# Attention and gated feed-forward on one core: the third query tile of two neighbouring head pairs by seven products over two query blocks

## The chip, the core and the metric

The kernel runs on one core of a Trainium2 chip. A core has a matrix engine (TensorE, PE in the profile, with its weight loads as PEld), a vector engine (VectorE, DVE), a scalar engine (ScalarE, ACT), a general engine (GpSimd, POOL) and a queue engine (SyncE, SP) that issues most transfers. The matrix engine writes its products to PSUM, eight banks of 512 float32 values in each of 128 partitions; everything else lies in SBUF or in the chip's main memory.

The metric is the device time in microseconds of one execution. A change is measured as the ratio of the times of the two kernels on the same chip.

## What is computed

`x` is 2048 rows of 640. It is normalized by rows (`xn`). Attention has 32 heads of width 192 and reads the last 512 rows of the key and value caches. The feed-forward part has a hidden width of 1536. Cut to what matters:

```python
xn = _layernorm(x)                                  # 2048 x 640
q = (xn @ wq).reshape(B, Sq, 32, 192)               # 32 heads
scores = einsum("bhqd,bhkd->bhqk", q, k[-512:]) * 192 ** -0.5
o = einsum("bhqk,bhkd->bhqd", softmax(scores), v[-512:])
s = o.reshape(B, Sq, 32 * 192) @ wo                 # 6144 x 640
g = silu((silu(xn @ w_gate) * (xn @ w_up)) @ w_down)
out = x + s * g
```

## The kernel before, in words

The work has three stages in time. First the feed-forward part over four blocks of 512 rows (to about 165 us), with the layer norm, the preparation of `wo` and of the first head pair beside it. Then the attention over 16 pairs of heads (to about 690 us). Then the output projection. The order of every engine's instructions is the order in which the code emits them: the scheduler is switched to manual.

**Attention.** Two heads have 384 columns of queries, that is three tiles of 128 columns (j = 0, 1, 2) for each of four blocks of 512 rows. A head pair has two halves of two blocks each. Each half is a *scores phase* (`scores_phase`) and a *stretch* of value products (`stretch`). A scores phase has eight slots. Each slot holds one group of six score matmuls (`scores`, L780, into one of two score tiles of two PSUM banks, read by an exponential on ScalarE, L789) and, ahead of it, some of the work that makes the queries of the *next* two blocks: blocks 2 and 3 of the same pair in the first half, blocks 0 and 1 of the next pair in the second. That work comes in units of ten matmuls of 64 rows by 512 columns; two of them run side by side in the two halves of the array. The products of a unit go to one of two tiles of two banks (`mm_tile`).

The first two query tiles of two blocks are not made by four products each (two row halves of `xn` by two column halves of the weights, for two blocks) but in the manner of Winograd's form of Strassen's scheme: seven products for eight. `q_diag` (L736, one unit for both groups of a pair), `differences` (L751), `sides` (L757), `across` (L763) and `sums` (L771) are its steps; the weights' sums come from `combine_wq` (L152, VectorE at L174, copies on GpSimd at L176 to L178), the sums of `xn` are made once (`xc`). One of the additions runs on GpSimd (L769). The third tile (j = 2) is made directly by `q_rows` (L711): two partial products over 64 rows each, which VectorE adds (L722). So a half has three units for the first two tiles and two for the third, and the first half has the diagonal unit of the next pair as a sixth, in slot 7.

Beside the slots (`beside`, L1060) go the transposes of the next pair's keys, their sums (`sum_k`, L200) and their centring (`centre_k`, L209 and L211), the loads of the pair after that (`load_k`, `load_wq`), and the spill of finished outputs to main memory (L868). The value products (L824) are divided on VectorE and ScalarE (`divide`, L847 and L853) and transposed by DMA (L859).

**The down projection** (`ffn_down`, L442) takes two row tiles at a time, also by seven products (W1 to W7) in three PSUM banks U, V, W out of four, which lie two by two in two tiles.

**The output projection** (`run`, L985) does the same with products M1 to M7 for eight pairs of row tiles; the last operations are products M3 into the bank of M5, two VectorE operations and a store.

Of the kernel before, what the change touches and what calls it, by code (L numbers as in the profile page):

```python
# [15 lines left out]
def kernel(  # L16
# [114 lines left out]
    BLOCKS = (slice(0, 6, 5), slice(2, 4), slice(1, 5, 3))  # L131
# [19 lines left out]

    def combine_wq(pr, step=0):  # L152

        rows = pairs[pr]["rows"]
        if step == 0:
            pairs[pr]["wq"] = wpool.tile([P, 5, NC, P], bf, name="wq_p", tag="wq_p")
        w = pairs[pr]["wq"]
        wc = pairs[pr]["wc"] = w[:, :, :, :].bitcast(h16)

        def part(of, r, n, t):  # L160
            return of[r, n, :, BLOCKS[t], :]

        def slot(of, r, n):
            return of[r, n, :, :].rearrange("p c (b d) -> p c b d", d=64)

        if pr == 0:
            for t in range(3):
                nc.vector.tensor_copy(out=slot(w, full, AS_IS[t]), in_=part(rows, full, 0, t))
            return
        if step < 2:  # L170
            r, own, other = ((lo, 1, 0), (hi, 0, 1))[step]
            a, b, c = part(rows, r, 0, own), part(rows, r, 0, other), part(rows, r, 1, other)
            for to, x, y, op in ((SWAP, c, a, ALU.add), (TOTAL, c, b, ALU.add), (OTHER, b, a, ALU.subtract)):
                nc.vector.tensor_tensor(slot(wc, r, to), x, y, op)  # L174
        else:
            nc.gpsimd.tensor_copy(out=slot(w, full, THIRD), in_=part(rows, full, 0, 2))  # L176
            nc.gpsimd.tensor_copy(out=slot(w, lo, OWN), in_=part(rows, lo, 0, 1))
            nc.gpsimd.tensor_copy(out=slot(w, hi, OWN), in_=part(rows, hi, 0, 0))  # L178

# [22 lines left out]
    CENTRE = [(0, lo, 0, lo), (0, hi, 2, hi), (1, full, 1, full), (2, lo, 0, hi), (2, hi, 2, lo)]  # L202
# [20 lines left out]
    def q_of(i, j):  # L223
        return q_pair(i)[:, 3 * (i % 2) + j, :]
# [4 lines left out]
    with ExitStack() as fctx:  # L229
# [212 lines left out]
        def ffn_down(b, u):  # L442
# [3 lines left out]
            at = 3 * (2 * b + u)  # L446
            U, V, W = (down_banks[(at + k) % 4] for k in range(3))
# [250 lines left out]

    pre = ctx.enter_context(tc.tile_pool(name="out_first", bufs=1, side="right"))
    ictx = ctx.enter_context(ExitStack())  # L700
    ppool = ictx.enter_context(tc.tile_pool(name="att_p", bufs=10, side="right"))
    opool = ictx.enter_context(tc.tile_pool(name="att_o", bufs=2, side="right"))
    otpool = ictx.enter_context(tc.tile_pool(name="att_ot", bufs=4, side="right"))
# [22 lines left out]
    DIAG_S, SIDE_S = 0, 1  # L726
# [9 lines left out]
    def q_diag(pr):  # L736

        ps, wc = mm_tile(), pairs[pr]["wc"]
        products(ps, [wc[:, SWAP, :, :]] * 2, [xc[:, DIAG, :, :]] * 2)
        nc.vector.tensor_copy(out=m_f[:, DIAG_S, :, :], in_=ps[:, :, :])  # L740

    def q_group(pr, g):
# [3 lines left out]
        st = {}  # L746

# [3 lines left out]
        def differences():  # L751
            st["own"] = mm_next[0]
            st["ps"] = mm_tile()
            w = pairs[pr]["wq"][:, OWN, :, :]
            products(st["ps"], [w] * 2, [xc[:, DIFF[g], :, :]] * 2)

        def sides():  # L757
            side = mm_tile(1 - st["own"])
            wc = pairs[pr]["wc"][:, TOTAL, :, :]
            products(side, [wc] * 2, [block(1), block(0)])  # L760
            nc.scalar.copy(m_f[:, SIDE_S, :, :], side[:, :, :])  # L761

        def across():  # L763
            nc.vector.tensor_tensor(  # L764
                q_pair(i)[:, 1:4:2, :], st["ps"][:, :, :], m_f[:, SIDE_S, ::-1, :], ALU.add
            )
            diag = m_f[:, DIAG_S, g : g + 1, :].to_broadcast([P, 2, 512])
            eng = nc.vector if pr == last else nc.gpsimd
            eng.tensor_tensor(m_f[:, SIDE_S, :, :], diag, m_f[:, SIDE_S, :, :], ALU.subtract)  # L769

        def sums():  # L771
            wc = pairs[pr]["wc"][:, OTHER, :, :]
            products(st["ps"], [wc] * 2, [xc[:, SUM[g], :, :]] * 2, first=False)
            nc.vector.tensor_tensor(
                q_pair(i)[:, 0:5:4, :], st["ps"][:, :, :], m_f[:, SIDE_S, :, :], ALU.add
            )

        return differences, sides, across, sums, lambda b: q_rows(i + b, 2, 1 - st["own"])
# [29 lines left out]
    def pv(i, q2, tile_of, by_dve):  # L808
# [3 lines left out]
        def part(p):  # L812
            if p == 0:
                if i not in OTs:
                    Obs[i] = O_late.pop(0) if i >= NS - 2 else opool.tile([P, 4, 2, Dh], bf, name="O_b")
                    OTs[i] = otpool.tile([P, 12, P], bf, name="OT_b")
# [89 lines left out]
    def load_a(n, q, cs=slice(0, KH), eng=nc.sync):  # L906
        side, k = divmod(q, 2)
        if (n, q) not in a_q:
            if n > 2 and n % 2:
                a_q[n, q] = a_q[n - 2, q]  # L910
            elif n == 1 and k == 0:
                pool, tag = ((wpool, "wq_p"), (wstage, "wq_rows"))[side]
                a_q[n, q] = pool.tile([P, KH, P], bf, name="a_q", tag=tag)
            else:
                pool = pre if n % 2 == 0 else wide
                a_q[n, q] = pool.tile([P, KH, P], bf, name="a_q", tag="a_q%d" % q)
# [8 lines left out]
    def a_sum(n, m):  # L925
        x, y, op = A_OF[m]
        third = len(a_s) % 3 == 2
        a_s[n, m] = (late[0] if third else qpool).tile(
            [P, KH, P], h16, name="a_s", tag="a_s" if third else "qT", bufs=1 if third else 2
        )  # L930

        def part(q):
            return a_s[n, q][:] if q in A_OF else a_q[n, q][:]

        nc.vector.tensor_tensor(a_s[n, m][:], part(x), part(y), op)

    def product(n, m, ps, first=True, ns=1):
        at = a_s[n, m] if (n, m) in a_s else a_q[n, A_OF[m][0]]
        w = HC // ns
        for k in range(ns):  # L940
            for c in range(KH):
                nc.tensor.matmul(  # L942
                    ps[k] if ns > 1 else ps, at[:, c, :], b_w[m][:, c, k * w : (k + 1) * w],
# [3 lines left out]
    def load_xg(n):  # L947
        for side, r in enumerate(ROW_PAIRS[n]):
            tag, bufs = ("khat", 2) if n % 2 == 0 else (("K_p", "KT")[side], 1)
            t = xg[n, side] = kpool.tile([P, 2, D], bf, name="xg", tag=tag, bufs=bufs)  # L950
# [34 lines left out]
    def run(n, m):  # L985
# [17 lines left out]
        elif m == M5:  # L1003
            ps = bank(n, "M5+M3")
            product(n, M5, ps)
            total(v, ps, v)
# [16 lines left out]
        else:  # L1023
# [4 lines left out]
            product(n, M3, ps, first=False)  # L1028
            if (n, m) == ORDER[-1]:
                total(c, ps, t[:, 1, last_cols], ALU.mult)  # L1030
                total(t[:, 0, last_cols], c, u)
                store(n, 0, last_cols, nc.scalar)
            else:
                total(u, ps, u)
# [12 lines left out]
        "0a0 s20 0b0 s21 0a1 s22 0b1 s23 1a0 s30 1b0 s31 1a1 s32 1b1 s33 "  # L1047
        "2a0 2b0 2a1 2b1 3a0 3b0 3a1 3b1"
# [11 lines left out]
    def beside(pr, n):  # L1060
# [11 lines left out]
        elif pr + 2 < NPAIR and n in (10, 12):  # L1072
            (load_k if n == 12 else load_wq)(pr + 2)
        half, n8 = divmod(n, 2 * KC)
# [21 lines left out]
    def scores_phase(pr, half):  # L1096


        nxt = pr + 1 < NPAIR
        if half == 0 and pr == 0:  # L1100
            work = [lambda i=i, j=j: q_rows(i, j) for i in (2, 3) for j in range(3)]
            slots = {0: work[0:1], 1: work[1:2], 3: work[2:3], 4: work[3:4], 5: work[4:5], 6: work[5:6]}
        elif half == 0 or nxt:
            of = pr if half == 0 else pr + 1
            differences, sides, across, sums, third = q_group(of, 1 - half)
            slots = {
                0: [differences], 1: [sides], 3: [across, lambda: third(0)], 4: [sums],
                6: [lambda: third(1)],
            }
        if half == 0 and nxt:  # L1110
            slots.setdefault(7, []).append(lambda: q_diag(pr + 1))
# [92 lines left out]
```

## Time and profile before

| what | us |
|---|---|
| median of three runs | 878.79 (878.28 to 879.32) |
| the profiled execution | 878.91 |
| its span, first to last instruction | 877.1 |
| TensorE clock granted | 1.00 throughout |
| PE busy, first stage (0 to 150) | 145.6 of 150 |
| PE busy, attention (300 to 600) | 299.9 of 300 |
| PE busy, end (800 to 877) | 73.5 of 77 |

The profile shows one execution. Busy time of an engine is the union of its instructions; since matmuls are pipelined, a busy PE is not PE at its peak. Durations of PE instructions include the way through the array, so that groups overlap; the pace is read from the starts. In lines of the timeline the columns are start, duration, engine, line, operation, tiles (out<-in), shapes and count, and in brackets the engine's idle time before it and what ended it.

### The profile page before, as it was taken

Reading aid. Unit: us, or ns where it says so; the run is one execution under the profiler, and the core shown is the slowest. Engines: PE = TensorE matmul, PEld = TensorE weight load, DVE = VectorE, ACT = ScalarE, POOL = GpSimd, SP = SyncE. Lnnn points to the kernel's source line nnn. Section 1 sums busy time; section 2 is a strip of 40 time slices with the busy share of each in tenths; the row PEclk is TensorE's granted clock in tenths of the full one; section 3 lists DMA queues with packets and bytes.
Section 4 is the critical chain, followed back from the end, with each engine's and each line's share of the span. In section 5 each row is a group of like instructions: output and inputs, shape, how many; then the busy total and the mean of one; then the engine's idle time right before and its main releaser. Section 6 shows DMA issues by size and latency. Waiting matters only on the chain.

```text
span 877.1 us, 22922 instructions
## 1 busy us (share of the span) xinstructions
PE 867.6 (99%) x9641; PEld 576.2 (66%) x9657; DVE 603.5 (69%) x1028; ACT 427.5 (49%) x649; POOL 114.2 (13%) x217
## 2 busy tenths in 40 slices
PE   8999999999999999999999999999999999999998
PEld 5455555567667667667667667667667777777775
DVE  6765876676876876876876876877775556555553
ACT  4264433665765765765765765765767300000000
POOL 0000000112122122122122132132120000000000
PEclk9999999999999999999999999999999999999999
DMA  9669974258999988977987777978899998645510
GB/s 294 172 210 275 214 222 116 67 98 180 204 204 217 201 179 200 195 162 176 198 177 179 176 149 163 208 165 189 167 230 251 255 355 294 212 171 176 176 54 16
DMA packets 273432, 165.52 MB, mean 189 GB/s; under 512 B 174384, under 2 KB 268208, under 8 KB 272816
## 3 DMA queue, kind: packets, MB, share of 16 engines
q1 hardware_dynamic: 271824, 156.08, 73.8%
q10 hardware_dynamic: 1504, 7.96, 2.6%
q8 instruction: 76, 1.25, 0.6%
q14 instruction: 28, 0.23, 0.1%
HBM read 89.95 MB, written 40.24 MB: 148 GB/s over the span
## 4 chain that ended last, share of the span: by engine, by line
PE 96%; DMA 1%; SPq 1%; DVE 1%; issue 0%; ACT 0%; ACTq 0%; DVEq 0%
PE acc L942 19%; PE sc L785 18%; PE mm L731 13%; PE sc L394 11%; PE mm L824 10%; PE sc L824 9%; PE mm L717 8%; PE mm L456 5%; PE sc L523 1%; DMA OT_b<-O_last 1%; DMA wg_sb<-in_B_w_gate_dram 1%; PE gu L394 0%; SPq L921 0%; DVE wq_p L174 0%; SPq L859 0%
## 5 line engine op out<-in xcount | busy, mean ns | idle before, releaser
L789 ACT ACTIVATE p_t<-sc 128x1024 bf16<-128x1024 f32 x256 | 253.6, 1024 | 59.8 <-PE sc L785 55.2
L785 PE MATMUL sc<-qT,khat 64*128 64x512 bf16 x1536 | 198.1, 376 | 0.0
L824 PEld LDWEIGHTS <-p_t 64*128 64x128 bf16 x4096 | 173.0, 94 | 8.6
L785 PEld LDWEIGHTS <-khat 64*128 64x128 bf16 x1536 | 89.0, 94 | 75.2 <-issue 0.5
L824 PE MATMUL mm<-V_p,p_t 64*128 64x193 bf16 x2112 | 111.6, 243 | 0.0
L824 PE MATMUL sc<-V_p,p_t 64*128 64x193 bf16 x1984 | 104.8, 243 | 0.0
L731 PE MATMUL mm<-xc,wq_p 64*128 64x512 f16 x750 | 94.4, 376 | 0.0
L942 PEld LDWEIGHTS <-a_s 128*128 128x128 f16 x768 | 75.1, 98 | 29.2
L731 PEld LDWEIGHTS <-wq_p 64*128 64x128 f16 (+1 forms) x1050 | 58.4, 94 | 47.9
L722 DVE TENSOR_REDUCE qT<-mm 128x512 bf16<-128x1024 f32 x66 | 80.6, 1222 | 13.0 <-PE mm L717 10.5
L769 POOL TENSOR_TENSOR m_f<-m_f 128x1024 f32<-128x1024 f32 x28 | 65.8, 2349 | 178.3 <-DVE qT L764 178.3
L853 ACT ACTIVATE O_b<-sc,r 128x192 bf16<-128x192 f32 x120 | 43.9, 419 | 86.7 <-PE sc L824 83.9
L717 PE MATMUL mm<-xnT,wq_p 64*128 64x512 bf16 x660 | 83.0, 376 | 0.5 <-DVE qT L722 0.4
L942 PE MATMUL acc<-b_w,a_q 128*128 128x320 bf16 (+1 forms) x576 | 81.8, 299 | 0.2 <-ACT xc L992 0.2
L942 PE MATMUL acc<-b_w,a_s 128*128 128x320 f16 (+1 forms) x576 | 81.8, 299 | 0.0
L992 ACT COPY xc<-acc 128x320 f32<-128x320 f32 x8 | 3.4, 428 | 141.5 <-PE acc L942 130.8
L942 PEld LDWEIGHTS <-a_q 128*128 128x128 bf16 x576 | 56.3, 98 | 22.3 <-issue 0.5
L394 PE MATMUL sc<-xnT,wg_sb 128*128 128x512 bf16 (+1 forms) x247 | 59.5, 353 | 2.1 <-DMA wg_sb<-in_B_w_gate_dram 1.1
L717 PEld LDWEIGHTS <-wq_p 64*128 64x128 bf16 x660 | 36.4, 94 | 36.8 <-issue 5.6
L401 ACT ACTIVATE sg<-sc 128x512 bf16<-128x512 f32 x46 | 27.3, 595 | 68.1 <-PE sc L394 66.3
L394 PE MATMUL sc<-xnT,wu_sb 128*128 128x512 bf16 (+1 forms) x260 | 60.3, 355 | 0.0
L764 DVE TENSOR_TENSOR qT<-mm,m_f 128x1024 bf16<-128x1024 f32 x30 | 36.7, 1224 | 31.9 <-ACT m_f L761 31.9
(110 smaller groups left out, 906.2 us busy)
## 6 DMA issues: line engine op xcount, KB each, us to landing
o_d<-OT_b SPq DMA_DIRECT2D x64, 384.0 KB, 5.6
a_q<-o_d SPq DMA_DIRECT2D x28, 768.0 KB, 5.9
won<-in_A_wo_dram SPq DMA_DIRECT2D x24, 320.0 KB, 4.2
wo_d<-wo_s SPq DMA_DIRECT2D x24, 320.0 KB, 2.7
wq_rows<-in_A_wq_dram SPq DMA_DIRECT2D x16, 480.0 KB, 4.8
wq_rows<-in_A_wq_dram SPq DMA_DIRECT2D x30, 240.0 KB, 5.8
K_p<-in_A_k_cache_dram SPq DMA_DIRECT2D x32, 192.0 KB, 5.8
V_p<-in_A_v_cache_dram SPq DMA_DIRECT2D x32, 192.0 KB, 3.2
```

The costliest lines, as they stand in the source:

```text
L394: nc.tensor.matmul(out, w_sb[:, c, f * P : (f + 1) * P], xnT[:, c, qc], start=(c == 0), stop=(c == NC - 1),)
L456: nc.tensor.matmul(ps, left[:, c, :], D_OF[m][:, c, :], start=(first and c == 0), stop=(c == KD - 1), skip_group_check=True,)
L717: nc.tensor.matmul(q_ps[:, h, :], w[r, AS_IS[j], c, :], xnT[r, c, b * 512 : (b + 1) * 512], start=(c == 0), stop=(c == NC - 1),)
L722: nc.vector.reduce_sum(q_of(i, j), q_ps[:, :, :].rearrange("p h n -> p n h"), axis=AX.X)
L731: nc.tensor.matmul(ps[:, h, :], ws[h][r, c, :], xs[h][r, c, :], start=(first and c == 0), stop=(c == NC - 1), skip_group_check=True,)
L764: nc.vector.tensor_tensor(q_pair(i)[:, 1:4:2, :], st["ps"][:, :, :], m_f[:, SIDE_S, ::-1, :], ALU.add)
L769: eng.tensor_tensor(m_f[:, SIDE_S, :, :], diag, m_f[:, SIDE_S, :, :], ALU.subtract)
L785: nc.tensor.matmul(sc[:, h, :], khat[r, j, ks], q_of(i, j)[r, :], start=(j == 0), stop=(j == 2))
L789: nc.scalar.activation(p_t[:, :, :], sc[:, :, :], ACT.Exp, scale=scale)
L824: m = nc.tensor.matmul(acc[:, k, h * 256 : h * 256 + Dh + 1], Ps[i][kc][r, h, qt * P : (qt + 1) * P], V_p[r, kc, h, 0 : Dh + 1], start=(p ...
L853: nc.scalar.activation(O_b[:, qt, h, :], a_k[:, h, 0:Dh], ACT.Copy, scale=r[:, k, h, :])
L942: nc.tensor.matmul(ps[k] if ns > 1 else ps, at[:, c, :], b_w[m][:, c, k * w : (k + 1) * w], start=(first and c == 0), stop=(c == KH - 1), ...
```

## The change

The third query tile is now also made by seven products, over the two blocks of a group and over *two neighbouring head pairs*: pairs 1 and 2, 3 and 4, up to 13 and 14 (`first_of_two`). Its weights are read again in the arrangement that this needs, six loads of 64 rows by 5 by 128 values (`load_third`), and combined by three VectorE sums of 128x640 (`combine_third`). The products for both pairs of such a duo are made in the scores phases that make the queries of the first of them. Pair 0 and pair 15 keep the direct form.

In the seven products themselves the first result (D, the differences) is now copied to SBUF by ScalarE; the second (`sides`) stays in PSUM, is added to D by VectorE, and takes the third (`sums`) on top. Before, the second was copied, and the first took the third on top. `across` is no longer a step of its own. For the third tile the additions write two half results each, since they belong to two pairs.

```diff
+    def load_third(pr):
+        w = new_wq(pr)
+        mine, next_ = (
+            wq[:, p * PD + 128 : p * PD + 256].rearrange("(c p) e -> p c e", p=P) for p in (pr, pr + 1)
+        )
+        for to, t_lo, t_hi in (
+            (w[:, THIRD, :, :], next_[lo], mine[hi]),
+            (third["rows"][:, 0, :, :], mine[lo], next_[hi]),
+            (third["rows"][:, 1, :, :], mine[hi], next_[lo]),
+        ):
+            nc.sync.dma_start(out=to[lo], in_=t_lo)
+            nc.sync.dma_start(out=to[hi], in_=t_hi)
+
+    def combine_third(pr):
+        own, same, swapped = pairs[pr]["wq"][:, THIRD, :, :], third["rows"][:, 0, :, :], third["rows"][:, 1, :, :]
+        for to, x, y, op in (
+            (SWAP, swapped, own, ALU.add), (TOTAL, swapped, same, ALU.add), (OTHER, own, same, ALU.subtract)
+        ):
+            nc.vector.tensor_tensor(third[to], x, y, op)
...
         def differences():
-            st["own"] = mm_next[0]
-            st["ps"] = mm_tile()
-            w = pairs[pr]["wq"][:, OWN, :, :]
-            products(st["ps"], [w] * 2, [xc[:, DIFF[g], :, :]] * 2)
+            st["x"] = mm_next[0]
+            ps = mm_tile()
+            products(ps, [own] * 2, [xc[:, DIFF[g], :, :]] * 2)
+            nc.scalar.copy(d, ps[:, :, :])
 
         def sides():
-            side = mm_tile(1 - st["own"])
-            wc = pairs[pr]["wc"][:, TOTAL, :, :]
-            products(side, [wc] * 2, [block(1), block(0)])
-            nc.scalar.copy(m_f[:, SIDE_S, :, :], side[:, :, :])
-
-        def across():
-            nc.vector.tensor_tensor(
-                q_pair(i)[:, 1:4:2, :], st["ps"][:, :, :], m_f[:, SIDE_S, ::-1, :], ALU.add
-            )
-            diag = m_f[:, DIAG_S, g : g + 1, :].to_broadcast([P, 2, 512])
+            ps = st["ps"] = mm_tile(st["x"] if of_third else 1 - st["x"])
+            products(ps, [wc[TOTAL]] * 2, [block(1), block(0)])
+            if of_third:
+                for h, to in enumerate((q_of(i + NB, 2), q_of(i + 1, 2))):
+                    nc.vector.tensor_tensor(to, ps[:, 1 - h, :], d[:, h, :], ALU.add)
+            else:
+                nc.vector.tensor_tensor(q_pair(i)[:, 1:4:2, :], ps[:, ::-1, :], d, ALU.add)
             eng = nc.vector if pr == last else nc.gpsimd
-            eng.tensor_tensor(m_f[:, SIDE_S, :, :], diag, m_f[:, SIDE_S, :, :], ALU.subtract)
+            eng.tensor_tensor(d, diag[:, g : g + 1, :].to_broadcast([P, 2, 512]), d, ALU.add)
 
         def sums():
-            wc = pairs[pr]["wc"][:, OTHER, :, :]
-            products(st["ps"], [wc] * 2, [xc[:, SUM[g], :, :]] * 2, first=False)
-            nc.vector.tensor_tensor(
-                q_pair(i)[:, 0:5:4, :], st["ps"][:, :, :], m_f[:, SIDE_S, :, :], ALU.add
-            )
+            ps = st["ps"]
+            products(ps, [wc[OTHER]] * 2, [xc[:, SUM[g], :, :]] * 2, first=False)
+            if of_third:
+                for h, to in enumerate((q_of(i, 2), q_of(i + NB + 1, 2))):
+                    nc.vector.tensor_tensor(to, d[:, h, :], ps[:, h, :], ALU.subtract)
+            else:
+                nc.vector.tensor_tensor(q_pair(i)[:, 0:5:4, :], d, ps[:, :, :], ALU.subtract)
```

The slots are filled anew. Of a pair that is the first of a duo both groups are made in a phase (slots 0, 1, 3 and 2, 4, 6); of the second pair only the first two tiles:

```diff
-            differences, sides, across, sums, third = q_group(of, 1 - half)
-            slots = {
-                0: [differences], 1: [sides], 3: [across, lambda: third(0)], 4: [sums],
-                6: [lambda: third(1)],
-            }
+            of, g = (pr, 1) if half == 0 else (pr + 1, 0)
+            differences, sides, sums, third_part = q_group(of, g)
+            if half and not first_of_two(of) and of < last:
+                slots[0].append(lambda: q_diag(of))
+            slots[0].append(differences)
+            slots[1].append(sides)
+            slots[3].append(sums)
+            if first_of_two(of):
+                differences, sides, sums, _ = q_group(of, g, True)
+                slots[2].append(differences)
+                slots[4].append(sides)
+                slots[6].append(sums)
+            elif of == last:
+                slots[2].append(lambda: third_part(0))
+                slots[5].append(lambda: third_part(1))
         if half == 0 and nxt:
-            slots.setdefault(7, []).append(lambda: q_diag(pr + 1))
-            slots.setdefault(2, []).extend(lambda k=k: combine_wq(pr + 1, k) for k in range(2))
-            slots.setdefault(5, []).append(lambda: combine_wq(pr + 1, 2))
+            slots[2].extend(lambda k=k: combine_wq(pr + 1, k) for k in range(2))
+            slots[5].append(lambda: combine_wq(pr + 1, 2))
+            if first_of_two(pr + 1):
+                slots[0 if pr else 4].insert(0, lambda: combine_third(pr + 1))
+                slots[2 if pr else 6].insert(0, lambda: q_diag(pr + 1, True))
+            if first_of_two(pr + 1) or pr + 1 == last:
+                slots[7].append(lambda: q_diag(pr + 1))
```

On VectorE's queue in the first phase of an odd pair this gives the order: add of the first group, six combining sums, subtraction of the first group, two adds of the third tile, two subtractions of the third tile. Before it was: six combining sums, add, direct sum, subtraction, direct sum, copy of the diagonal.

A tile `third` in SBUF holds the new weights, D, the diagonal and the second pair's queries. The exponentials have nine buffers for ten and the transposed outputs three for four (the last block's lies in `K_p`), and the output projection's tiles lie elsewhere: `a_q` in `third`, sums of `a_q` in halves in the two `khat` tiles, `xg` in `V_p` and `third`. The order of the last pair's scores among its value products is changed.

In the down projection the banks are fixed, and U and V always lie in different tiles:

```diff
-            at = 3 * (2 * b + u)
-            U, V, W = (down_banks[(at + k) % 4] for k in range(3))
+            U, V, W = (down_banks[k] for k in ((0, 2, 3), (1, 3, 2))[u])
```

In the output projection the very last M5 and M3 are made in two halves of 160 columns in two banks, and finished and stored by halves, on two queues:

```diff
+                pss = [ps, acc[n, "M5+M3'"]]
+                product(n, M3, pss, first=False)
+                w = HC // len(pss)
+                for k, ps in enumerate(pss):
+                    part, cols = slice(k * w, (k + 1) * w), slice(HC + k * w, HC + (k + 1) * w)
+                    total(c[:, part], ps[:, 0:w], t[:, 1, cols], ALU.mult)
+                    total(t[:, 0, cols], c[:, part], u[:, part])
+                    store(n, 0, cols, (nc.sync, nc.scalar)[k])
```

## The prediction

> **What bounds the kernel now.** I read the page's busy table and chain first, then the stretches of one head pair, then the timeline of that pair, then the end.
>
> ```profile
> span 877.1 us, 22922 instructions
> PE 867.6 (99%) x9641; PEld 576.2 (66%) x9657; DVE 603.5 (69%) x1028; ACT 427.5 (49%) x649; POOL 114.2 (13%) x217
> ...
> PE 96%; DMA 1%; SPq 1%; DVE 1%; issue 0%; ACT 0%; ACTq 0%; DVEq 0%
> ```
>
> PE is the bound in every stage: a change gains what it takes from PE's queue, as long as PE waits for nobody new. The stretches of pair 7 (two scores phases, each followed by its value products) and what runs beside them:
>
> ```profile
> 399.44:411.13 11.69, 11.69 (x114) 6.16 (x111) 8.79 (x14) 9.22 (x12) 4.38 (x4) 1.00 0.93 202
> 411.13:416.46 5.33, 5.33 (x130) 5.33 (x128) 3.06 (x8) 1.75 (x3) 0.39 (x4) 1.00 0.47 98
> 416.46:427.07 10.61, 10.61 (x103) 5.66 (x100) 9.07 (x14) 8.56 (x12) 2.35 (x1) 1.00 0.83 166
> 427.07:432.44 5.37, 5.37 (x131) 5.34 (x128) 3.56 (x10) 2.30 (x4) 0.40 (x4) 1.00 1.19 311
> ```
>
> Columns: length, then busy time of PE, PEld, DVE, ACT, POOL, granted clock (1.00), DMA share. The first phase has six units of q work (a unit is ten 64-row matmuls), the second five, each has eight score groups: a unit is 11.69 - 10.61 = 1.08 us, a score group (10.61 - 5 x 1.08) / 8 = 0.65. PE is never idle. ACT is at 9.2 of 11.7, DVE at 8.8: their slack is small, and the even mixing of units and scores is what lets them keep up. From the timeline (start, duration; in brackets idle time before):
>
> ```profile
> 400.36 2.59 DVE L174 TENSOR_TENSOR wq_p<-wq_rows 64x640 f16<-64x640 bf16 x6
> 403.56 1.23 DVE L764 TENSOR_TENSOR qT<-mm,m_f 128x1024 bf16<-128x1024 f32 x1 [0.61 <-ACT m_f L761]
> 404.86 2.34 POOL L769 TENSOR_TENSOR m_f<-m_f 128x1024 f32<-128x1024 f32 x1 [6.36 <-DVE qT L764]
> ...
> 417.57 0.73 ACT L853 ACTIVATE O_b<-sc,r 128x192 bf16<-128x192 f32 x2
> 419.54 1.01 ACT L761 COPY m_f<-mm 128x1024 f32<-128x1024 f32 x1
> 420.45 1.95 ACT L789 ACTIVATE p_t<-sc 128x1024 bf16<-128x1024 f32 x2
> 421.89 2.35 POOL L769 TENSOR_TENSOR m_f<-m_f 128x1024 f32<-128x1024 f32 x1 [6.36 <-DVE qT L764]
> 423.03 1.23 DVE L209 TENSOR_SCALAR nmean<-ssum 128x3 f32<-128x3 f32 x1
> ```
>
> The reader is to see three things. The six combining sums (L174) run before POOL's operation, at a time when POOL is idle. POOL's operation starts as L764 ends. And L209, three elements wide, takes 1.23 us: it ends at 424.26, POOL's operation at 424.24. A DVE instruction that reads only SBUF was held until POOL was done (in the table of lines from 300 to 660 us all eleven of them have a mean of 1128 ns, and the 512 wide centring next to them 349). The other direction, earlier in the trace:
>
> ```profile
> 161.82 0.69 DVE L543 TENSOR_TENSOR xc<-xnT,xc 64x1024 f16<-64x1024 bf16 x1
> ...
> 162.17 0.91 POOL L176 COPY wq_p<-wq_rows 128x640 bf16<-128x640 bf16 x1 [67.23 <-PE mm L456]
> ```
>
> L543 adds two SBUF tensors, as the combining sums do; the POOL copy that met it took 0.91, where the group's mean in the attention part is 720 ns.
>
> **The change, part by part.** Pairs 1 and 2, 3 and 4, up to 13 and 14 make seven duos. *PE work.* The third tile's 8 direct units of a duo become 7: 7 x 1.08 = 7.5 us less. But the units move: I call the phases of a duo A (odd pair, first), B (odd, second), C (even, first), D (even, second). Units before: 6, 5, 6, 5; after: 6 (two groups of three), 4, 5, 6. I walk each phase through the queues in the new order, time zero at its first unit, with the durations above; the same walk of the kernel before gives 11.6 and 10.5 for the measured 11.69 and 10.61.
>
> *A.* Units in slots 0, 1, 2, 3, 4, 6. The sides' products end at 3.0, the add (1.23) runs to 4.25. Before, the combining sums stood ahead of it in DVE's queue; now they stand behind it, and POOL's operation starts at the same moment. No row shows two-tensor sums beside this POOL operation, so I bound it. Overlapping freely: sums to 6.8, POOL to 6.65, the subtraction (L774's 1.22) to 8.0, the two new half-width adds (0.69 each, the row of 128x512 products with a PSUM operand, L402) to 9.5; PE, ready for the last unit at 9.25, waits 0.3. Held like L209 and L176: 4.25 + 2.59 + 2.35 = 9.2, subtraction to 10.35, adds to 11.7, and PE waits 2.45. I take held, as the row nearest in kind (L543 against L176) and the clearest (L209) both show it: A is +2.5. Behind the wait stand the last unit, two scores and the value products.
>
> *B.* Four units, diag and differences both in slot 0, and five scores in a row. ACT finishes O_b at 1.9, copies D when the second unit is out (2.5 to 3.5), and its first exponential starts at 3.45, where it started at 1.9 before. Two score banks: a score waits for the exponential two before it, so PE goes at about 0.98 (0.65 + 1.02 + latencies 0.29, halved) instead of 0.65: scores 5, 6, 7 start at 8.55, 9.5, 10.5, and B ends at 11.15, +0.55 in spite of one unit less. This has no port in it.
>
> *C.* Units in slots 0, 1, 2, 3, 7. POOL runs 4.3 to 6.65, DVE's copy of the new diagonal 4.75 to 6.0, then the combining sums wait and run 6.65 to 9.2, the subtraction to 10.4. The slot 7 unit needs the bank which this frees; PE is there at 9.8. End about 12.4, +0.8. Overlapping freely the scores alone set 11.5: -0.15. If POOL's two waiting copies (0.72 each) take turns with the sums, another 1.4.
>
> *D.* Six units for five, +1.08; the new adds stand behind the subtraction, which waits for POOL (6.65), and behind L209 and the first centring: 8.4 to 9.75 against PE's 9.25, +0.35 with its rounding: +1.4.
>
> Sum of phases: 7 x 2.5 + 7 x 0.55 + 6 x 0.8 + 7 x 1.4 = 36.0 (C of pairs 2 to 12; D follows pairs 0 to 12; pair 14 about even). The very first phase gains a unit (+1.08) and three sums (1.3) on a DVE that already makes PE wait 0.37 there: +2. In these walks are the two extra copies of D per duo on ACT (0.91 from start to start) and the two extra POOL operations, against two POOL copies (0.72) less.
>
> The Trainium skill, "SBUF — State Buffer", section "SBUF: two separate sides", says that GpSimd and a VectorE operation with two SBUF inputs exclude each other for a whole instruction. The 1.23 of L209 and the 0.91 of L176 agree; by that rule the sum is as taken, without it A and C fall to their free ends.
>
> *Loads.* Six 80 KB loads per duo on SP's queue, in B: 6 x 0.64 (L148's three take 1.91) = 3.8 us, ahead of the second spill. SP idles from 427.7 to 430.6 there, so the O_b transposes start up to 0.9 late, and next V_p (issued 402, landing 3.2 later, needed at 411) and KT (issued 404.6, summed at 417.4). Covered. The rows themselves (issue to 429, landing 5.8) come at about 434.8, the first user at 434.2; the add waits for 3.0 into the phase. Nothing taken; uncovered, 7 x 0.7.
>
> *Down projection.* Products W1 and W2 use halves of one PSUM tile in every even unit; it shows only where no hidden products lie between:
>
> ```profile
> 149.74 0.98 PE L456 MATMUL mm<-wd_sb,hT 128*128 128x320 bf16 x6 [0.57 <-ACT qT L478]
> 151.37 0.97 PE L456 MATMUL mm<-wq_p,khat 128*128 128x320 f16 x6 [0.65 <-DVE qT L462]
> ```
>
> In the next unit, with U and V in different tiles, W1 and W2 run on without a gap (157.60, x12). The new banks always differ: -1.2.
>
> *Last columns.* 48 matmuls of 160 columns for 24 of 320 in M5 and M3: 128-column ones start every 56 ns in the first stage, so columns, not weights, set the pace: 0. Behind the last product, two DVE operations of 0.49 become half as wide: -0.5 at most (0.3 to 0.5), bound 0. The reordered last pair and the room for a_q, a_s and xg: same count of products; last exponential to its reader 1.33 of cover against 1.02 + 0.2: 0, bound +1. Nine p_t for ten: eight are live, and a phase's first exponential comes behind the value products that free one. Three OT_b for four: the reused one's spill was issued a phase before and lands in 5.5. Both 0.
>
> Total 36.0 + 2 - 1.2 - 0.5 = +36.3: span 877.1 + 36.3 = 913.4. The profiled execution took 878.91, its span plus 1.8; the median is 878.79. So 915.1.
>
> **Rivals.** (1) *No exclusion:* A +0.3, B +0.55, C -0.15, D +1.4: 2.1 + 3.9 - 0.9 + 9.8 + 2 - 1.7 = +15.2, 894. For it: no trace row has these two side by side. Against: L209, eleven times. (2) *Turns:* C +1.4 six times, 923.5. For it: POOL's request would be the older one. Against: L174's six follow each other without a gap. (3) *Faster:* PE never waits, because ACT and DVE, with 11 and 8.5 us idle in each 33, run ahead as they do now: -7.5 - 1.2 - 0.5 = -9.2, 869.6. It decides where the waits of a duo stay below 1.08 us (about 0.3 in A, 0.3 in D, under 0.5 in B and C together); B alone has 1.6 in my walk, so the walk would have to be wrong about the two score banks.
>
> **How the numbers follow.** Held 0.46 (915), turns 0.16 (924), free 0.24 (894), faster 0.10 (870), 0.04 for anything else. Likeliest 915. The range 888 to 928 holds the first three, with the late rows (+5) above 924 and an error of 6 in B and D below 894. About 0.2% (1.8 us) is what a measurement tells from no change: faster 0.10, same 0.02, slower 0.88.
>
> **What would show it.** In the profile after: phases A, B, C, D of 14.2, 11.2, 12.4, 12.0; PE idle before the third tile's last unit in A, released by DVE's half-width add; sums L180 either starting as POOL ends, or POOL's operation starting as they end; L209's counterpart short in D. If A is under 12.2 while the sums lie beside POOL's operation, the exclusion is wrong and 894 is near; if B is under 10, the walk is wrong and the time falls below 885.

## The result and the profile after

The changed kernel takes 936.31 us (median of 4 runs, 934.53 to 942.61), the kernel before beside it 878.56: ratio 1.0668, 95% interval 1.065 to 1.0687. Forecast was 915, range 888 to 928. The sign was right; the loss is 57.5 us of span (934.6 against 877.1) instead of 36.3. Busy table and chain of the page of the changed kernel:

```profile
span 934.6 us, 23150 instructions
PE 880.5 (94%) x9619; PEld 572.0 (61%) x9635; DVE 619.7 (66%) x1075; ACT 439.2 (47%) x663; POOL 144.1 (15%) x217
...
PE 72%; DVE 13%; issue 8%; ACT 2%; POOL 2%; DMA 1%; SPq 1%; ACTq 0%; DVEq 0%; POOLq 0%
```

The trace has fewer matmuls than before (9619 against 9641), and PE is busy longer, 880.5 against 867.6: as shown below, some of them ran slower. The chain, 96% PE before, now has DVE in 13%. PE's waits, from the view of waits (us in total, times, the longest):

```profile
PE mm L779 <- DVE qT L814: 16.5, 14, 2.1
PE sc L836 <- ACT p_t L840: 10.7, 24, 0.5
PE mm L779 <- DVE qT L827: 10.1, 6, 2.3
PE mm L779 <- DVE qT L770: 3.7, 1, 3.7
PE acc L1010 <- ACT O_last L907: 2.1, 1, 2.1
```

In this order they are: the third tile's last unit in A (2.11 each) and D (0.25 each), the scores, mostly in B and C, the last unit in C, one wait in the very first phase, and one at the start of the output stage. The four phases of the duo of pairs 7 and 8 (length, busy time of PE, PEld, DVE, ACT, POOL, granted clock, DMA share, GB/s):

```profile
427.28:441.23 13.95, 11.84 (x114) 6.10 (x111) 9.35 (x13) 9.48 (x13) 4.81 (x2) 1.00 0.86 197
446.94:458.28 11.34, 10.36 (x92) 4.87 (x90) 8.24 (x15) 8.89 (x12) 2.35 (x1) 1.00 0.93 175
463.62:476.89 13.27, 11.10 (x103) 5.47 (x100) 10.57 (x16) 9.10 (x12) 4.14 (x3) 1.00 1.08 231
482.23:494.32 12.09, 11.83 (x114) 6.11 (x111) 9.20 (x14) 9.48 (x13) 4.65 (x2) 1.00 0.93 177
```

Forecast were 14.2, 11.15, 12.4 and 12.0. All duos show the same but for A, which is 13.94 four times and 15.6 three times (pairs 1, 5, 11), and C of pair 12, 15.60. Phase A of pair 7 in the timeline:

```profile
430.38 1.23 DVE L816 TENSOR_TENSOR qT<-mm,m_f 128x1024 bf16<-128x1024 f32 x1 [2.09 <-PE mm L779]
431.52 4.85 DVE L180 TENSOR_TENSOR wq_p<-wq_rows 64x640 f16<-64x640 bf16 x6
431.68 2.53 POOL L818 TENSOR_TENSOR m_f<-m_f 128x1024 f32<-128x1024 f32 x1 [5.33 <-DVE qT L816]
...
436.38 1.22 DVE L827 TENSOR_TENSOR qT<-m_f,mm 128x1024 bf16<-128x1024 f32 x1
437.52 0.68 DVE L814 TENSOR_TENSOR third<-mm,third 128x512 bf16<-128x512 f32 x1
438.12 0.68 DVE L814 TENSOR_TENSOR qT<-mm,third 128x512 bf16<-128x512 f32 x1
438.86 1.26 PE L779 MATMUL mm<-xc,third 64*128 64x512 f16 x10 [2.11 <-DVE qT L814]
```

The six sums took 2.59 before and take 4.85 now; taken one by one in phase A of pair 3, five of them take 0.48 and the second 2.55: it starts 0.32 after POOL's operation and ends 0.35 after it. The subtraction (L827), the half-width adds (L814) and PE follow one behind the other, as forecast; PE waits 2.11 for the 2.45 said.

The 1.66 us that three of the A phases have on top are a lower granted clock. The stretches around the wait of pair 5 (it falls into the first of these) and the one of pair 9:

```profile
362.44:365.85 3.41, 1.30 (x14) 0.59 (x12) 2.64 (x4) 1.94 (x2) 0.61 (x1) 1.00 1.01 293
365.85:369.26 3.41, 3.41 (x20) 1.45 (x18) 1.28 (x2) 1.02 (x1) 3.10 (x3) 0.50 0.22 83
509.21:512.62 3.41, 1.37 (x14) 0.74 (x15) 1.99 (x3) 1.32 (x2) 1.28 (x1) 1.00 0.61 205
512.62:516.04 3.42, 3.26 (x62) 2.49 (x60) 1.29 (x2) 1.94 (x2) 2.63 (x5) 1.00 0.00 0
```

The records of the clock show 0.50 for exactly 3.41 us, five times before the end (from 178.11, 219.07, 365.85, 584.30 and 621.85), and 1.00 everywhere else; the kernel before has none. All starts lie on one grid of 3.413 us (12, 43, 64 and 11 steps apart). In pair 5 the whole wait of 2.11 falls into one step of that grid, and the next step runs at half speed. In pair 9 the grid cuts the same wait, 2.05 of idle time lie in one step, and nothing follows. The four runs of this kernel differ in the same way: 942.61, 936.47, 936.14 and 934.53 us come with a mean granted clock of 0.987, 0.991, 0.991 and 0.995. At 1.71 us of clock lost in each stretch that is about seven, five, five and three stretches, an estimate from the means.

The budget by stages in us, from the starts and ends of phases in both traces (the measured terms sum to 57.5):

| term | forecast | measured |
|---|---|---|
| A, seven | +17.5 | +15.4 at full clock, +5.0 of half clock |
| B, seven | +3.9 | +5.1 |
| C of pairs 2 to 12 | +4.8 | +7.9 in five, +3.9 in pair 12 (half clock in it) |
| D, seven | +9.8 | +10.2 |
| very first phase | +2 | +6.6 (half clock in it) |
| last unit phases of pairs 14 and 15 | 0 | +1.4 |
| value products behind the phases | 0 | +1.4 |
| last pair, to the output stage | 0 | +3.1 (19.05 against 15.99) |
| down projection, with the start-up | -1.2 | -2.05 |
| output stage | -0.5 | -0.5 |

### The profile page after: what moved, and what is told of

Read it like the earlier page. It is cut to its first block, busy times and chain, and to the rows that moved or that the text cites. A ratio compares the mean times of both kernels' runs of the same rounds, so it can differ in the third digit from the quotient of the medians.

```text
span 934.6 us, 23150 instructions
## 1 busy us (share of the span) xinstructions
PE 880.5 (94%) x9619; PEld 572.0 (61%) x9635; DVE 619.7 (66%) x1075; ACT 439.2 (47%) x663; POOL 144.1 (15%) x217
## 3 DMA queue, kind: packets, MB, share of 16 engines
q8 instruction: 75, 1.23, 0.6%
## 4 chain that ended last, share of the span: by engine, by line
PE 72%; DVE 13%; issue 8%; ACT 2%; POOL 2%; DMA 1%; SPq 1%; ACTq 0%; DVEq 0%; POOLq 0%
PE acc L1010 20%; PE mm L779 11%; PE sc L431 11%; PE mm L878 9%; PE sc L878 8%; PE sc L836 8%; DVE wq_p L180 5%; PE mm L492 5%; DVE qT L827 3%; ACT p_t L840 2%; POOL m_f L818 2%; DVE qT L816 1%; PE mm L765 1%; DVE third L814 1%; DVE qT L814 1%
## 5 line engine op out<-in xcount | busy, mean ns | idle before, releaser
L836 PE MATMUL sc<-qT,khat 64*128 64x512 bf16 x1312 | 185.2, 383 | 12.0 <-ACT p_t L840 10.7
L878 PEld LDWEIGHTS <-p_t 64*128 64x128 bf16 x4096 | 172.7, 94 | 12.5 <-issue 2.6
L779 PE MATMUL mm<-xc,wq_p 64*128 64x512 f16 x890 | 112.8, 379 | 10.8 <-DVE qT L827 10.1
L779 PEld LDWEIGHTS <-wq_p 64*128 64x128 f16 (+1 forms) x1190 | 65.3, 94 | 71.0 <-issue 17.5
L1010 PEld LDWEIGHTS <-a_s 128*128 128x128 f16 x816 | 77.2, 98 | 27.4
L1010 PE MATMUL acc<-b_w,a_s 128*128 128x320 f16 (+2 forms) x600 | 81.9, 294 | 0.0
L180 DVE TENSOR_TENSOR wq_p<-wq_rows 64x640 f16<-64x640 bf16 x90 | 68.9, 791 | 0.8
L896 DVE RECIPROCAL r<-mm 128x4 f32<-128x4 f32 x66 | 12.0, 182 | 74.4 <-PE mm L878 74.1
L1010 PE MATMUL acc<-b_w,a_q 128*128 128x320 bf16 (+1 forms) x384 | 54.8, 299 | 2.1 <-ACT O_last L907 2.1
L439 DVE TENSOR_TENSOR hT<-sc,sg 128x512 bf16<-128x512 f32 x46 | 31.7, 690 | 35.2 <-ACT sg L438 35.1
L901 DVE TENSOR_TENSOR O_b<-mm,r 128x384 bf16<-128x384 f32 x98 | 51.5, 554 | 2.2
```

The costliest lines, as they stand in the source:

```text
L779: nc.tensor.matmul(ps[:, h, :], ws[h][r, c, :], xs[h][r, c, :], start=(first and c == 0), stop=(c == NC - 1), skip_group_check=True,)
L836: nc.tensor.matmul(sc[:, h, :], khat[r, j, ks], q_of(i, j)[r, :], start=(j == 0), stop=(j == 2))
L878: m = nc.tensor.matmul(acc[:, k, h * 256 : h * 256 + Dh + 1], Ps[i][kc][r, h, qt * P : (qt + 1) * P], V_p[r, kc, h, 0 : Dh + 1], start=(p ...
L901: nc.vector.tensor_tensor(O_b[:, qt, :, :], a_k[:, :, 0:Dh], r[:, k, :, :].to_broadcast([P, 2, Dh]), ALU.mult,)
L1010: nc.tensor.matmul(ps[:, 0:w], at[c], b_w[m][:, c, k * w : (k + 1) * w], start=(first and c == 0), stop=(c == KH - 1), skip_group_check=True,)
```

## The experiments

**Sums first.** The six combining sums are put ahead of the add in DVE's queue.

```
-            slots[2].extend(lambda k=k: combine_wq(pr + 1, k) for k in range(2))
+            slots[0 if pr else 2][:0] = [lambda k=k: combine_wq(pr + 1, k) for k in range(2)]
```

> The changed kernel with the six combining sums given to VectorE at the head of the phase, ahead of the first group's add, instead of behind it (phases A and C; in C behind the third tile's three sums). Nothing else moves. Theory (VectorE's two-input sums and POOL's operation exclude each other, and the half-clock windows are the answer to a wait of PE of over 2 us): A goes from 13.94 (15.6 where a window fell) to about 12.4 and has no window left, C from 13.27 to about 12.9; 7 x 1.5 + 3 x 1.66 + 5 x 0.4, about 18 us: 918. Rival (A is long because ACT and the two score banks set its pace, as in B): the order on VectorE does nothing, A stays 13.9, 936.

Measured: 919.97 us, ratio to the kernel before 1.0459 (1.044 to 1.0477), 16 us faster than the changed kernel. A is 12.27 seven times, C 12.57 to 12.59, but 13.19 and 16.63 in pairs 4 and 12: there VectorE waits 0.5 and 2.3 for the third rows at the head of the phase, and the six sums now stand behind that wait (in pair 12 a half-clock stretch follows). Phase A of pair 7, timeline:

```profile
418.98 2.78 DVE L180 TENSOR_TENSOR wq_p<-wq_rows 64x640 f16<-64x640 bf16 x6
...
421.79 1.23 DVE L816 TENSOR_TENSOR qT<-mm,m_f 128x1024 bf16<-128x1024 f32 x1
...
423.10 2.35 POOL L818 TENSOR_TENSOR m_f<-m_f 128x1024 f32<-128x1024 f32 x1 [5.97 <-DVE qT L816]
...
427.95 1.26 PE L779 MATMUL mm<-xc,third 64*128 64x512 f16 x10 [0.44 <-DVE qT L814]
```

The sums take 2.78 again, POOL's operation 2.35, and PE waits 0.44 for 2.11. No half-clock stretch lies in any A. The queue's order decides, and the rival falls.

**POOL's operation on VectorE.** Here the order stays and the other partner of the exclusion goes.

```
-            eng = nc.vector if pr == last else nc.gpsimd
-            eng.tensor_tensor(d, diag[...], d, ALU.add)
+            nc.vector.tensor_tensor(d, diag[...], d, ALU.add)
```

> The changed kernel with POOL's operation (diagonal plus D) given to VectorE in all pairs. Theory (exclusion): VectorE gets 1.23 us more in each group, but the sums and the operation no longer wait for another engine's turn: A about 13.2, C about 12.5, fewer half-clock windows: 7 x 0.7 + 6 x 0.8 + up to 5 us of clock, 920 to 930, faster than the changed kernel. Rival (it is the amount of work in VectorE's queue, not the exclusion): A and C get longer by 1.2 each, 13 x 1.2, so 950.

Measured: 917.71, ratio 1.0442 (1.041 to 1.0474). A 13.16, C 12.46, no half clock in any phase. VectorE does 1.23 us more in every group, and yet A and C get shorter (C of pair 12, with its late rows, is 13.01; B stays at 11.35): what VectorE lost before was time in which it was held. The six sums take 2.79, and PE's wait in A falls from 2.11 to 1.33. The phases came out as expected, and the whole is 2 us under the 920 to 930 expected, although this run gives 5 us back later: PE waits 3.6 once in the output stage for a_s, whose sum stands on DVE behind a late load of xg. Why that load is late was not tried.

**Third rows later, in the first phase.**

```
+            if half and of == 1:
+                slots[0].append(lambda: q_diag(of, True))
...
-                slots[0 if pr else 4].insert(0, lambda: combine_third(pr + 1))
-                slots[2 if pr else 6].insert(0, lambda: q_diag(pr + 1, True))
+                slots[0 if pr else 7].insert(0 if pr else len(slots[7]), lambda: combine_third(pr + 1))
+                if pr:
+                    slots[2].insert(0, lambda: q_diag(pr + 1, True))
```

The lines that it answers are these of the changed kernel's timeline, first phase:

```profile
176.11 0.49 DVE L212 TENSOR_TENSOR third<-third,wq_p 128x640 f16<-128x640 bf16 x1 [3.19 <-DMA third<-in_A_wq_dram]
...
177.32 2.35 DVE L770 TENSOR_REDUCE qT<-mm 128x512 bf16<-128x1024 f32 x2
178.59 2.31 PE L779 MATMUL mm<-xc,third 64*128 64x512 f16 x10 [3.72 <-DVE qT L770]
```

VectorE stands idle for 3.19 until a load lands, two reductions wait behind it with their inputs ready, PE waits 3.72, and the unit then takes 2.31 instead of 1.26, at half clock.

> The changed kernel with the first duo's combining of the third rows moved from slot 4 of the very first phase to its end, and its diagonal unit from slot 6 there to the head of the next phase. Theory (the rows land late, at about 176, VectorE waits 3.2 for them with PE's reductions queued behind it, PE then waits 3.7 and a half-clock window follows): the first phase goes from 20.0 to about 14.5, the window at 178 is gone, the next phase grows by one unit (1.08): about -4.4, 932. Rival (the wait is not the rows' but the seven units' in VectorE's queue): the wait only moves, the two phases together keep their 32 us, 935 to 937.

Measured: 931.39, ratio 1.0597 (1.0569 to 1.0625), 4.9 faster than the changed kernel. The four runs of each kernel differ by more than that (929.35 to 934.76 here), so the phases decide: the first goes from 19.97 to 13.56, the next from 12.07 to 13.29, and the wait is gone from the trace. The late rows, not the count of units, made it.

**The two ends alone, on the kernel before.** Down projection banks and halves of the last columns, nothing of the attention.

```
-            at = 3 * (2 * b + u)
-            U, V, W = (down_banks[(at + k) % 4] for k in range(3))
+            U, V, W = (down_banks[k] for k in ((0, 2, 3), (1, 3, 2))[u])
```

> The kernel before, with two parts of the change alone: the down projection's other banks, and the last product in halves of 160 columns with two stores. Theory (these two are independent of the pairs): down projection -2.0 as the changed kernel showed, end -0.4: 876.2 against 878.6. Rival (what is won in the down projection is lost again in the first phase, whose start waits for something that keeps its time): within 0.5 of the kernel before.

Measured: 877.3 us in 11 runs, ratio 0.9974 (0.9964 to 0.9984): faster than both kernels. The result lies between theory and rival. Of the down projection's -2.05 in the changed kernel, 0.51 had come before it, since the first loads landed earlier in that run; in this one they landed later (+0.88 at the same place, -0.67 behind the down projection). Both traces give 1.55 for the banks. From its first product to the last VectorE operation the output stage takes 184.0 here, 184.1 in the kernel before and 183.6 in the changed kernel. So the split of the last columns alone is worth 0.1; the rest of the 0.5 in the changed kernel stands beside its other changes to the output stage, and no run took them apart.

**The same work in another order.** All units of the phases are spread (the order stands in the expectation); no instruction is added or left out.

> The changed kernel with the same instructions in another order. A: combining sums at the head, differences in slot 0, sides and the third tile's differences in slot 1, its sides in 3, sums in 4, its sums in 6. B: diagonal 0, differences 2, sides 4, sums 6. C: combining sums at the head, differences 0, POOL's two copies 1, sides 2, sums 4, the third rows' sums 5, the two diagonals 6 and 7. D as A. The first duo's third rows as in the run with the rows later. Theory (all of the loss is order: waits behind the exclusion, the two score banks in B, late rows, and the clock windows that the waits bring): A 11.7, B 9.9, C 11.3, D 11.7, no half-clock window up to the last pair; 7 x (2.9 + 1.5 + 1.9 + 0.4) + 5 + 1.3 is 53 off 936: 880 to 884. Rival (part of it is the scheme's own work: two more copies on ACT and two more operations on POOL per duo): the walk's 65.8 per duo is not reached, B stays over 11 whatever the order, 890 or more.

Measured: 881.74 us in 6 runs, ratio 1.0041 (1.0026 to 1.0055). The duo of pairs 7 and 8, same columns as above:

```profile
400.40:412.09 11.69, 11.69 (x114) 6.21 (x110) 8.38 (x15) 9.47 (x14) 5.97 (x4) 1.00 0.91 199
417.51:427.43 9.92, 9.92 (x93) 4.89 (x91) 8.09 (x12) 8.46 (x12) 2.35 (x1) 1.00 0.87 170
432.79:444.06 11.27, 11.18 (x103) 5.48 (x99) 8.47 (x16) 8.99 (x12) 2.93 (x2) 1.00 1.13 225
449.39:461.05 11.66, 11.66 (x114) 6.21 (x110) 9.02 (x13) 9.37 (x13) 4.71 (x2) 1.00 0.92 176
```

PE is busy in 44.45 of 44.54 us, with the same ACT copies and POOL operations as in the changed kernel. So 55.4 of the 57.5 us of span were order (879.2 against 934.6). The lengths sum to 44.54 against 44.60 before (11.69 and 10.61 twice): the 1.08 that each duo saves goes in B, where four units and eight scores are 9.5 and take 9.92, and in C, where five units take 11.27 and took 10.61. These are stops too short to show as idle time, since a matmul's duration includes its way through the array; the starts show them: in B it is 1.45 and 1.57 from the start of the first and the third pair of scores to what follows them, 1.29 and 1.30 from the other two. What makes them was not tried.

**Without the pairing of pairs.** Which part of the change brought the bad order? Here every pair makes its third tile directly, as before; D in SBUF, the add, POOL's operation and the sums stay where the change put them. POOL copies the direct weights again, and every pair has its diagonal unit in slot 7.

```
     def first_of_two(pr):
-        return pr % 2 == 1 and pr + 1 < NPAIR
+        return False
...
-            elif of == last:
+            else:
                 slots[2].append(lambda: third_part(0))
                 slots[5].append(lambda: third_part(1))
```

> The changed kernel without the pairing of pairs: every pair makes its third tile directly, in slots 2 and 5, and its diagonal unit in slot 7, as the last pair does; D copied to SBUF, the add, POOL's operation and the sums in slots 0, 1, 3 stay, and so do the new banks of the down projection and the last columns. Theory (what costs is the new order of one pair's own group, sums behind the add and POOL beside them): the first phase of a pair is about 14.6 (11.69 before), the second 11.2 (10.61): 14.5 x 3.5, about 50 us slower than the kernel before, 925 to 935, though no third tile is made of two pairs. Rival (it is the third tile of two pairs that costs): with that gone the phases are those of the kernel before, 877 to 880.

Measured: 934.36, ratio 1.0624 (1.058 to 1.0669). The first phase is 13.80 at full clock (14.6 was forecast) and the second 11.28. The headline part of the change, the third tile of two pairs, is absent, and the loss is about the same. Stretches on the clock's grid in pairs 6, 7 and 10:

```profile
395.79:399.20 3.41, 1.09 (x12) 0.45 (x9) 3.36 (x5) 1.63 (x2) 0.01 (x1) 1.00 0.60 188
399.20:402.61 3.41, 3.41 (x32) 2.43 (x30) 1.46 (x2) 1.02 (x1) 0.04 (x1) 0.50 0.00 0
433.34:436.75 3.41, 1.45 (x16) 0.65 (x12) 3.37 (x5) 1.84 (x2) 0.00 (x0) 1.00 0.89 253
436.75:440.16 3.41, 3.41 (x35) 2.52 (x31) 1.32 (x2) 1.02 (x1) 0.10 (x1) 0.50 0.01 5
545.98:549.39 3.41, 1.45 (x16) 0.79 (x15) 3.17 (x5) 1.43 (x2) 0.00 (x0) 1.00 0.36 111
549.39:552.81 3.42, 3.42 (x82) 3.22 (x77) 1.96 (x4) 1.02 (x1) 0.20 (x2) 1.00 0.00 0
```

Half speed comes in eight pairs on end (2 to 9), 37.55 us or 11 steps of the grid apart: with the loss in it, a pair is as long as 11 steps, so the next wait lies on the grid as the last one did. In pair 10 the step has the same 1.45 of busy time, and no half speed follows; why is open.

**Without the pairing, in a better order.** Sums at the head, direct units in slots 3 and 6, the group's sums in 4.

> The run without the pairing of pairs, with the combining sums at the head of the first phase, the direct units in slots 3 and 6 and the sums in slot 4. Theory: first phase 11.9, second 10.8, about 0.5 per pair over the kernel before, less 1.5 of the down projection: 884. Rival (copying D costs by itself, as ACT has it on the way of its exponentials): over 895.

Measured: 888.01, ratio 1.0107 (1.0093 to 1.0121). First phase 11.92, second 10.84, as forecast. The time is 4 over the 884 expected: the last pair adds its 3 us, and a half-clock stretch follows its last wait, at the head of the output stage (185.2 instead of 183.6). The rival (over 895) falls: D in SBUF costs 0.46 per pair in this order.

**The last pair.** The spread kernel, with the last pair's interleaving and units in the order of the kernel before.

> The run with the units spread, and in addition the last pair as in the kernel before: its score groups and value products interleaved in the old order, its direct units in slots 3 and 6 and its sums in 4. Theory (the changed kernel's last pair costs 3.0 from its first value product to the output stage, 19.0 against 16.0, by its new interleaving, and its two phases 0.7 each): 881.7 - 3.0 - 1.4 = 877.4, faster than the kernel before by 0.1%. Rival (the 3.0 come from the smaller stock of p_t, nine for ten, or from the PSUM bank that the first output product gets, not from the order): only the 1.4 are won, 880.3.

Measured: 880.22 us in 12 runs (878.63 to 888.01), ratio 1.0028 (1.001 to 1.0047). The theory missed; the rival's time came out, though its sum did not: the wait before the output stage is gone, but the last pair takes 18.2 instead of 19.0 (16.0 before), and its phases win 0.6, not 1.4. In its place PE waits twice 0.92 for an exponential that waits for a free p_t. So the stock of p_t was tried alone:

```
-    ppool = ictx.enter_context(tc.tile_pool(name="att_p", bufs=10, side="right"))
+    ppool = ictx.enter_context(tc.tile_pool(name="att_p", bufs=9, side="right"))
```

> The kernel before with nine buffers for p_t instead of ten, nothing else. Theory (the last pair's interleaving holds eight and makes two more before it frees any): two waits of PE of about 1 us each in the last pair, 18.2 for its interleaving instead of 16.0, +2.2: 881.0. Rival (nine are enough, as forecast): 878.8.

Measured: 880.28 us in 10 runs, ratio to the kernel before 1.0015 (1.0005 to 1.0024). The last pair takes 18.19 for 15.99, as expected, by these two waits in the timeline. The whole rises by less than the 2.2 expected; in the traces the span is 1.3 longer, as this run starts its first phase 0.47 earlier and the trace of the kernel before has short stops of 0.45 in two phases.

```profile
679.33 0.82 PE L785 MATMUL sc<-qT,khat 64*128 64x512 bf16 x6 [0.92 <-ACT p_t L789]
...
685.69 0.82 PE L785 MATMUL sc<-qT,khat 64*128 64x512 bf16 x6 [0.92 <-ACT p_t L789]
```

**Turns.** POOL's two copies ahead of its operation in C.

```
-            slots[5].append(lambda: combine_wq(pr + 1, 2))
+            slots[0 if pr and first_of_two(pr + 1) else 5].insert(0, lambda: combine_wq(pr + 1, 2))
```

> The changed kernel with POOL's two copies of the next pair's rows ahead of POOL's operation in phase C (pairs 2 to 12), where they run as the phase begins, instead of behind it. Theory (turns: a POOL copy waits for a sum and a sum for a copy, and the two copies stretch the six sums by 1.4, less what they overlap): C goes from 13.27 to about 12.5, the length that was forecast without turns; 6 x 0.8, about 931. Rival (C is long because of its late third rows and VectorE's copy of the diagonal): C keeps 13.2, 936.

Measured: 928.23 (2 runs), ratio 1.056 (1.0539 to 1.0581). C is 12.50 to 12.52 in five pairs and 12.80 in pair 12: the theory holds and the rival falls. In the changed kernel, C of pair 8:

```profile
468.01 2.35 POOL L818 TENSOR_TENSOR m_f<-m_f 128x1024 f32<-128x1024 f32 x1 [5.33 <-DVE qT L816]
...
469.51 4.35 DVE L180 TENSOR_TENSOR wq_p<-wq_rows 64x640 f16<-64x640 bf16 x6
470.30 0.98 POOL L184 COPY wq_p<-wq_rows 64x640 bf16<-64x640 bf16 x1
471.34 0.88 POOL L185 COPY wq_p<-wq_rows 64x640 bf16<-64x640 bf16 x1
```

With the copies ahead, the sums take 3.60 there and the copies 0.71 and 0.72. Copy, sum, copy, sum went in turns, and that cost 0.77 per C. A keeps 13.94 and its wait of 2.11 in this run, yet no A has a half-clock stretch: no step of the grid holds over 2.05 of one. Of the 8.0 us of span won, C of six pairs has 6.6, pair 12's half clock in it; the half clock of A, 5.0, is gone too, and the start, the value products and the output stage (185.2 for 183.6, with a half-clock stretch at its head) give the rest back.

## Why the forecast was right and where it failed

- **What bounds it, and the exclusion: right.** "Held like L209 and L176" gave A 14.2; it is 13.94 at full clock. Taking away either partner shortens PE's wait of 2.11, to 0.44 with the sums first and to 1.33 with the operation on VectorE, and the six sums then take 2.8 instead of 4.85. L209's successor is short in D, 162 ns on average, as said, but the 128-partition centring behind it is held in its place: 2.34 us in D of pair 8, where 0.35 is its mean in the kernel before. The Trainium skill (page "SBUF — State Buffer", section "SBUF: two separate sides") calls it an exclusive lock that goes to whoever starts first, for a whole instruction; the sum of 2.55 us that ends 0.35 after POOL's operation agrees.
- **B and D: right.** 11.35 for 11.15, 12.08 for 12.0. The two score banks set B: spreading its four units over slots 0, 2, 4, 6 brought it to 9.92, with the same work in it.
- **The step that failed most: a sum with no term for the granted clock.** The loss is 21.2 us over the forecast. I priced each wait at its own length. Five stretches of half clock follow waits of over 2 us: three in A (1.66 each, by 15.6 against 13.94), one in the first phase, one in C of pair 12; if each costs the same, 8.3 us. The other large terms, turns in C, late rows and the last pair, stand below; each is 3 to 5. The kernel before, with a clock of 1.00 up to its last store, couldn't show it. The Trainium skill has the rule (page "TensorE: Matmul & The Clock Gate", Part 1): a free-running window of 3413 ns, and half rate after an idle one. The grid of 3.413 us agrees; "idle" differs, since here PE was busy for up to 1.45 of the 3.41. It should have been a rival of its own for every wait of 2 us.
- **The loads, "Covered" and "Nothing taken": wrong at one place, small at another.** The rows of the first duo land at about 176, DVE waits 3.19 and PE 3.72: 5 us with the clock, as the run with the rows later shows. I saw that DVE "already makes PE wait 0.37 there", and priced the unit and the sums (+2), not the wait of a queue for a DMA. In C of pair 12 the rows are late too.
- **C: copies that "take turns with the sums, another 1.4", and I took none.** They do, and it is 0.77 per C, 4.6 in six; without the turns C is 12.5, against the 12.4 forecast. The forecast had this as its rival (2), held and with turns, at 923.5 and a chance of 0.16.
- **The reordered last pair at "0, bound +1" and "Nine p_t for ten" at 0: wrong.** Nine cost 2.2 in the last pair with the old interleaving, and the new one costs 3.1: 2.1 before the first output product, which waits for ACT's last division, the rest in shorter waits. I had counted live tiles in an ordinary phase and not in the last pair, which in the old order makes three p_t before it frees the first.
- **Down projection: right**, 1.55 for 1.2. **Last columns:** 0.1 alone, for 0.5 taken, inside the bound of 0 to 0.5.
- **Rival (3), faster because ACT and DVE run ahead:** false for this order, but with the units spread PE shows no wait over 0.15 in a duo, and even so the phases only come to 44.54 against 44.60.

The fastest version of all is the kernel before with the two ends, 877.3, by 0.26%.

## What to carry to other kernels

Count an edit's units, but price the order: here the same instructions took 936 or 882 us. Before a VectorE sum and a GpSimd operation are put side by side, move the one that is ready first to where the other engine is idle, and keep anything that waits for a load out of a queue that others are behind. Here a wait of PE of 2.11 us cost up to 1.66 more than its length, and no step of the clock's grid with under 1.96 of idle time had this price. So keep single waits well below that.

## What the hardware showed that I had not expected

Up to the last product, the half clock always lasts 3.41 us and starts on a grid that runs through a whole trace. Seven traces have it there: the changed kernel, sums first, operation on VectorE, rows later, copies first, and the two without the pairing. In these it followed every step with 2.08 us or more of idle PE, and none with less than 1.96. Between these it isn't idle time alone that decides: 2.00 and 2.05 had no effect in the changed kernel, while in the kernel without pairing 1.96 to 1.98 had one seven times and 1.96 none twice (the stretches above show 1.45 of busy time with both outcomes). What else counts was not tried. So the same wait of 2.11 costs 2.1 or 3.8 by where it falls, and the loop whose length with the loss in it was 11 steps of 3.413 us paid it eight times on end.
